# Top-k attention with a PReLU layer behind it: GpSimd's two row operations made one per tile, VectorE's product search moved by a slot

## The chip, the core and the metric

The kernel runs on one core of a Trainium2 chip. A core has a matrix engine (TensorE, in the profile PE, its weight loads PEld), VectorE (DVE), ScalarE (ACT), GpSimd (POOL), and SyncE (SP), whose instructions here only start DMAs. Each engine takes its instructions in program order and waits on semaphores where it needs what another engine makes. The metric is device time in microseconds (us): the median of a few executions. Before the change it is 826.78 us (three runs, 823.99 to 827.34).

## The reference

Two stages follow each other. Attention over 64 (batch, head) pairs, with 576 queries and 576 keys of 64 numbers each, in which every query keeps only the scores that are at least its 32nd largest:

```python
scores = scale * np.matmul(q, k.transpose(0, 1, 3, 2))
kth = np.partition(scores, -top_k, axis=-1)[..., -top_k:-top_k + 1]
mask = scores >= kth
scores = np.where(mask, scores, -1000000000.0)
scores = scores - np.max(scores, axis=-1, keepdims=True)
attn = np.exp(scores)
attn = attn / (np.sum(attn, axis=-1, keepdims=True) + 1e-09)
return np.matmul(attn, v)
```

Then a layer over 4608 tokens: `h = x @ w_in`, `g = max(h, 0) + alpha * min(h, 0)`, `out = g @ w_out`, with 512 inputs, 2048 hidden and 512 outputs.

## The kernel before

**Tiles.** The scores are made in tiles of 128 partitions with two rows of 576 scores on each. The code calls such a tile a duo: two rows (`i` = 0 and 1), each with a threshold of its own per partition. There are ND = 144 duos. One pass of the main loop (`for n in range(ND)`) is a slot, and in slot n every stage works on another duo, so that the duos run through the engines as through a pipeline. Two neighbouring duos 2m and 2m+1 form a group m, whose thresholds are found together.

**How a threshold is found.** ScalarE copies the scores of a duo out of PSUM into the tile `s` (`st_exit`). VectorE's MAX8 instruction gives the 8 largest of a row. It is run over six pieces of 96 scores of each row, 12 times for a duo. From these candidates, in odd slots, `fold`, `negate`, `least` and `turn` make a first threshold for the four rows of the group; it goes to column 0 of the tile `p9`. ScalarE counts the scores above it with a sign function whose sum is kept (`st_count`, tile `sg`, counts `cs`). GpSimd multiplies scores and signs (`st_y`, tile `y`), and VectorE's MAX8 over a row of `y` (`row(d, i)`) brings the 8 scores that lie next beside the threshold. With the count, three small VectorE instructions (`pick_steps`: `eq_`, `pk_`, `kt_`) pick the exact 32nd largest, and `kt_` writes it to columns of `KT`, which lies in the tile `KZ` of the profile. ScalarE then makes a penalty for every score below it (`st_relu`, tile `r`, which reads `KT`), GpSimd subtracts it from `s` in place, and ScalarE takes the exponential into the tile `w` (`st_exp`). A DMA transposes `w` into `wT`, and TensorE multiplies it with the values.

**What a slot does, in order, on each engine.** In slot n:

- ScalarE: sign of both rows of duo n-2; exponential of n-5; now and then a copy of finished output (`o_act`); penalty of both rows of n-4; exit of n+1; now and then a copy of transposed inputs (`qkT`).
- GpSimd: products of both rows of n-2; subtraction of both rows of n-4; in many slots a cast of values to bf16 (`cast_v`).
- VectorE, even slots: 12 MAX8 over duo n, with `eq_`, `pk_`, `kt_` of group (n-4)/2 behind the 2nd, 4th and 6th; the activation of the layer (`h_relu`, tile `gT`); row 0 of duo n-2; the reciprocal (`norm_a`); row 1 of duo n-2; the scaling of an attention output (`norm_b`); now and then a copy of transposed inputs.
- VectorE, odd slots: 12 MAX8 over duo n; `fold`, `h_relu`, `negate`; row 0 of duo n-2; `least`, `turn`; row 1 of duo n-2.
- TensorE: scores of duo n+1, attention output of an older duo, pieces of the layer, and matmuls over zeros (`rest<-idle`) where there is no work.

**What sets the order.** The order within each engine is that of the program text (class `Ordered`; the profile therefore puts nearly all instructions at line 32). What runs in which slot is a table by hand, `stage`, made from lags: `("count", 2)` means that duo d is counted in slot d+2, `("relu", 4)` that its penalty comes in slot d+4, `("exp", 5)` its exponential in slot d+5; picks of group m come in slot 2m+4. `dve_slot` is VectorE's part of a slot. In its present form it takes the rows from the table's `"count"` entries, that is in slot d+2. The scores of one duo lie in a single PSUM tile, so that TensorE makes the next scores only after the exit.

**Behind the loop** the last duos are finished in straight code: the last count and product of duo 142 (`st_count(D - 1)`, `st_y(D - 1)`), the picks of group 70, then `h_relu`, masks on VectorE for the last four duos (`st_mask`), and what is left of the layer.

Of the kernel before, what the change touches and what calls it, by code (L numbers as in the profile page):

```python
# [9 lines left out]
BF16 = mybir.dt.bfloat16  # L10
I32 = mybir.dt.int32
AF = mybir.ActivationFunctionType
ALU = mybir.AluOpType
# [3 lines left out]
BIG = float(2.0 ** 60)  # L17
# [42 lines left out]
def fast_path(tc, q, k, v, moe_w_in, moe_w_out, moe_alpha, out, flag):  # L60
    nc = tc.nc
    B, H, S, D = q.shape
# [9 lines left out]
    PE, ACT, DVE, POOL, SP = (  # L72
        Ordered(tc, e) for e in (nc.tensor, nc.scalar, nc.vector, nc.gpsimd, nc.sync)
    )
# [18 lines left out]
    with ExitStack() as ctx:  # L93
# [6 lines left out]
        two = pool("two", 2)  # L100
# [45 lines left out]
        def sm(ins, reads, writes):  # L146


            meet = lambda x, y: x == y if str in (type(x), type(y)) else x[0] < y[1] and y[0] < x[1]
            hit = lambda a, b: any(meet(x, y) for x in a for y in b)  # L150
            keep = [r[0] for r in recent
                    if hit(writes, r[1]) or hit(writes, r[2]) or hit(reads, r[2])]
            tc.declare_no_dep(ins.ins, group="small", keep=keep, reason="other columns")
            tc.add_to_no_dep_group("small", ins.ins)
            DVE.small.add(ins.ins.name)
            recent.append((ins.ins, reads, writes))
            del recent[:-60]
# [7 lines left out]
        KT = KZ[:, 0:2 * ND]  # L165
# [66 lines left out]
        T = {}  # L232
# [32 lines left out]
        def norm_of(n):  # L265

            return stage.get(("norm", n), 0)

        def pick_steps(m):

            def eq_():
                sm(DVE.tensor_tensor(eq, io9.unsqueeze(1).to_broadcast([128, 4, 9]),
                                     T.pop(("cs", m)).unsqueeze(2).to_broadcast([128, 4, 9]), ALU.is_equal),
                   [(292, 301)], [(256, 292)])

            def pk_():
                pk = T["pk"] = two.tile([128, 4, 9], FP32, name="pk", tag="pk")
                sm(DVE.scalar_tensor_tensor(out=pk, in0=eq, scalar=BIG, in1=T.pop(("p9", m)), op0=ALU.mult,
                                            op1=ALU.mult), [(256, 292), f"p9{m % 3}"], ["pk"])

            def kt_():
                sm(DVE.tensor_reduce(out=KT[:, 4 * m:4 * m + 4].unsqueeze(2), in_=T.pop("pk"),
                                     op=ALU.add, axis=AX.X), ["pk"], [])
            return [eq_, pk_, kt_]

        def row(d, i):
            DVE.max(out=T["p9", d // 2][:, 2 * (d % 2) + i, 1:9], in_=T["y", d][:, i, :])
# [29 lines left out]
        def dve_slot(n, f_late):  # L317

            norm = norm_of(n)
            rows = duos_at("count", n)  # L320
            picks = [f for m in duos_at("pick", n) for f in pick_steps(m)]
            s = T["s", n]
            if n % 2 == 0:
                T["up", n // 2] = two.tile([128, 4, NG // 2, 8], FP32, name="up", tag="up")
            up = T["up", n // 2]
            for i in range(2):
                r = 2 * (n % 2) + i
                for g in range(NG):
                    o = 24 * r + 8 * (g // 2)
                    m = DVE.max(out=(lo if g % 2 else up)[:, r, g // 2, :],  # L330
                                in_=s[:, i, GW * g:GW * g + GW])
                    if g % 2:
                        sm(m, [], [(o, o + 8)])
                        if picks:
                            picks.pop(0)()
            turn = None
            if n % 2:
                fold, negate, least, turn = threshold_steps(n // 2)
                fold()
                h_relu()  # L340
                negate()
            else:
                h_relu()
            for d in rows:
                row(d, 0)
            if turn:
                least()
                turn()
            if norm:
                norm_a(norm)  # L350
            for d in rows:
                row(d, 1)
            if norm:
                norm_b(norm)
            if f_late:
                h_pe()
                h_relu()
# [3 lines left out]
        def duos_at(kind, n):  # L361
            return stage.get((kind, n), [])

        for d in range(ND):
            for kind, lag in (("count", 2), ("relu", 4), ("exp", 5), ("av", 8 if d < 13 else 7)):
                stage.setdefault((kind, d + lag), []).append(d)
        for m in range(ND // 2):
            stage["pick", 2 * m + 4] = [m]
# [15 lines left out]
        def st_y(n):  # L384
            y = two.tile([128, 2, S], FP32, name="y", tag="y")
            sg = T.pop(("sg", n))
            for i in range(2):
                POOL.tensor_tensor(y[:, i, :], T["s", n][:, i, :], sg[:, i, :], ALU.mult)
            T["y", n] = y

        def st_relu(n, i):
            s = T["s", n]
            if i == 0:
                T["r", n] = two.tile([128, 2, S], BF16, name="r", tag="sg", bufs=3)
            r = T["r", n]
            ACT.activation(r[:, i, :], s[:, i, :], AF.Relu, bias=KT[:, 2 * n + i:2 * n + i + 1], scale=-BIG)
            POOL.tensor_tensor(s[:, i, :], s[:, i, :], r[:, i, :], ALU.subtract)

        def st_exp(n):
            w = ws[n % 3]  # L400
# [38 lines left out]
        def norm_a(n):  # L439
            rz = RZ[:, 2 * n - 2:2 * n + 2].rearrange("p (a h) -> p a h", a=2)  # L440
            DVE.reciprocal(rz, T["xo", n // 2][:, :, :, 64])
            T["rz"] = rz
# [112 lines left out]
        def h_relu(eng=None):  # L555
            if act:
                ch, f0, e_n, ph = act.pop(0)
                if eng is ACT:
                    ACT.activation(ch["g"][:, f0:f0 + e_n, :], ph, AF.Relu)
                else:  # L560
                    DVE.tensor_scalar(ch["g"][:, f0:f0 + e_n, :], ph, 0.0, None, ALU.max)
                ch["done"] += e_n
# [151 lines left out]
        for n in range(ND):  # L714
            now[0] = n
            run(n, "ld")
            o_sp()

            if not h_pe():
                keep_warm()  # L720
            wide_copy = n % 2 and (n, "prep") in todo
            if n > 3:
                run(n, "prep", 1)
            if n and on(n + 1):
                st_qk(n + 1)
            if n < 4:
                run(n, "prep", 2)
            for m in duos_at("av", n):
                st_av(m)
            late = len(hq) > (9 if n < 118 else 4) and n % 2 == 0  # L730

            for m in duos_at("count", n):
                st_count(m)
                st_y(m)
            for m in duos_at("exp", n):
                st_exp(m)
            if ready() > 4 or not wide_copy:
                o_act()
            did = o_pe()
            run(n, "w")  # L740

            dve_slot(n, late)
            for m in duos_at("relu", n):
                st_relu(m, 0)
                st_relu(m, 1)
            if on(n + 1):
                st_exit(n + 1)
            run(n, "cast")
            run(n, "lin_out")
            if (n, "lin") in todo:  # L750
                run(n, "lin")
            elif not ready() > 2 or not o_pe():
                if not did:
                    keep_warm()
            while pend:
                short = len(pend[0][0].shape) == 3
                wide = pend[0][0].shape[1] == 512
                on_dve = n > 3 and (short and n > 16 or wide and (n < 17 or n % 2 == 0))
                prep_evac(DVE.tensor_copy if on_dve else ACT.copy)
            if n == 1:  # L760
                sm(DVE.tensor_copy(alpha_ps, aps), [], [(304, 320)])
                ACT.activation(alpha1m, aps, AF.Copy, scale=-1.0, bias=1.0)
            run(n, "scale")
            if norm_of(n):
                st_xT(norm_of(n) - 1)
                st_xT(norm_of(n))

        def picked(m):
            for f in pick_steps(m):
                f()  # L770
            kv = T["kv", m] = two.tile([128, 4], FP32, name="kv", tag="kv")
            DVE.tensor_scalar(kv, KT[:, 4 * m:4 * m + 4], 1.0 / BIG, None, ALU.mult)
# [25 lines left out]
        D = ND - 1  # L798
# [5 lines left out]
        h_pe(2)  # L804
        st_count(D - 1)
        st_y(D - 1)
        picked(D // 2 - 1)
        h_relu()
        normed(D - 6)
# [46 lines left out]
        turn = 0  # L856
# [296 lines left out]
```

## Time and profile before

| what | value |
|---|---|
| median of three runs | 826.78 us |
| the profiled execution, its own time | 825.79 us |
| its span, first to last instruction | 823.8 us |
| granted TensorE clock, mean | 0.989 |

The profile is of a single execution. Its span is 2.0 us shorter than that execution's own time. The page gives busy time by engine, the chain of work that ended last, groups of equal instructions with their mean duration and the idle time before them, and DMA queues. Other views of the same trace list instructions in order of time, waits by who ended them, and busy time in chosen stretches. A row "x2" in a list by time is two instructions merged, with the time from the start of the first to the end of the last. On VectorE and ScalarE the recorded durations of neighbours overlap by some 0.1 us, so that the step from one start to the next is shorter than a duration.

### The profile page before, as it was taken

To read this page: it belongs to the slowest core of one execution; us is meant where nothing else is said; L and a number is where in the kernel's file an instruction comes from. 1 tells how busy PE (TensorE), PEld (TensorE's weight loads), DVE (VectorE), ACT (ScalarE), POOL (GpSimd) and SP (SyncE) were. 2 spreads that over 40 slices of the span, in tenths; PEclk is the share of its full clock that TensorE was granted. 3 is DMA by queue.
4 is the path that set the end of the run, shared out by engine and by line. 5 is a ranking of instruction groups with operands and counts; after the bars stand their busy time and mean duration, and the time that the engine had idled before them with its cause. 6 is when DMAs were issued, how large, how long until landed. Compare 5 with 4: busy or idle time off the path is not lost.

```text
span 823.8 us, 17880 instructions
## 1 busy us (share of the span) xinstructions
PE 742.5 (90%) x5422; PEld 424.1 (51%) x5422; DVE 760.5 (92%) x3474; ACT 763.4 (93%) x1258; POOL 745.4 (90%) x700
## 2 busy tenths in 40 slices
PE   8878889999899898998989898898989899989886
PEld 5333445555555555555545454455545555555554
DVE  3999989999999999999999999999999999999961
ACT  4999989999999999999999999999999998999921
POOL 1899989999998999999999999999999998999810
PEclk9999999999999999999999999999999999999989
DMA  6699977555666656556656556566666555544351
GB/s 138 171 184 179 176 132 144 104 121 116 123 131 125 122 102 139 109 130 124 132 109 141 112 94 142 119 135 113 117 134 123 123 93 110 92 88 87 69 119 43
DMA packets 344168, 100.21 MB, mean 122 GB/s; under 512 B 338032, under 2 KB 338048, under 8 KB 344064
## 3 DMA queue, kind: packets, MB, share of 16 engines
q1 hardware_dynamic: 340992, 91.87, 56.8%
q0 software_dynamic: 1872, 6.82, 3.5%
q8 instruction: 45, 0.74, 0.4%
q14 instruction: 59, 0.48, 0.2%
q10 hardware_dynamic: 1200, 0.30, 0.2%
HBM read 36.71 MB, written 9.44 MB: 56 GB/s over the span
## 4 chain that ended last, share of the span: by engine, by line
DVE 40%; ACT 19%; PE 19%; POOL 12%; issue 6%; DMA 2%; SPq 1%; ACTq 0%; POOLq 0%
DVE small L32 12%; DVE p L32 10%; DVE up L32 7%; POOL y L32 6%; ACT r L32 5%; POOL s_sb L32 5%; ACT sg L32 5%; PE ps_sc L32 5%; DVE gT L32 5%; ACT s_sb L32 4%; PE pz L32 4%; PE ph L32 4%; ACT w L32 3%; PE xo L32 2%; DVE qkT L32 2%
## 5 line engine op out<-in xcount | busy, mean ns | idle before, releaser
L32 POOL TENSOR_TENSOR y<-s_sb,sg 128x576 f32<-128x576 f32 x288 | 362.6, 1278 | 34.6 <-ACT sg L32 34.1
L32 POOL TENSOR_TENSOR s_sb<-s_sb,r 128x576 f32<-128x576 f32 x280 | 352.1, 1278 | 6.1 <-ACT r L32 5.8
L32 ACT ACTIVATE sg<-s_sb,p 128x576 bf16<-128x576 f32 x288 | 221.4, 773 | 6.9 <-DVE p L32 5.5
L32 DVE MAX8 up<-s_sb 128x8 f32<-128x96 f32 x864 | 212.6, 246 | 10.4 <-ACT s_sb L32 10.4
L32 DVE MAX8 p<-y 128x8 f32<-128x576 f32 x288 | 215.0, 748 | 6.4 <-POOL y L32 5.9
L32 DVE MAX8 small<-s_sb 128x8 f32<-128x96 f32 x864 | 216.8, 251 | 0.0
L32 PE MATMUL ps_sc<-qkT 64*128 64x512 f32 (+2 forms) x768 | 182.1, 563 | 23.2 <-ACT s_sb L32 23.1
L32 ACT ACTIVATE r<-s_sb,KZ 128x576 bf16<-128x576 f32 x280 | 201.0, 768 | 0.3 <-DVE KZ L32 0.3
L32 ACT COPY s_sb<-ps_sc 128x1152 f32<-128x1152 f32 x144 | 159.1, 1105 | 11.4 <-PE ps_sc L32 11.1
L32 ACT ACTIVATE w<-s_sb 128x1152 bf16<-128x1152 f32 x140 | 161.7, 1155 | 1.2 <-POOL s_sb L32 1.0
L32 PE MATMUL ph<-xT,w_in_b 128*128 128x256 bf16 (+1 forms) x1472 | 150.4, 250 | 6.8 <-DVE gT L32 3.3
L32 PEld LDWEIGHTS <-w_in_b 128*128 128x128 bf16 x1472 | 120.6, 98 | 50.0 <-issue 12.9
L32 PE MATMUL pz<-w_out_b,gT 128*128 128x512 bf16 x544 | 140.6, 381 | 0.4 <-DVE gT L32 0.4
L32 PE MATMUL xo<-v,wT 128*128 128x65 bf16 (+1 forms) x1560 | 123.4, 198 | 2.4 <-DMA wT<-w 2.1
L32 PEld LDWEIGHTS <-wT 128*128 128x128 bf16 (+3 forms) x1600 | 97.7, 100 | 32.7 <-DMA wT<-w 3.3
L32 DVE TENSOR_SCALAR gT<-ph 128x512 bf16<-128x512 f32 x137 | 92.5, 675 | 10.0 <-PE ph L32 10.0
L32 PEld LDWEIGHTS <-gT 128*128 128x128 bf16 x576 | 56.1, 98 | 71.1 <-issue 16.8
L32 PEld LDWEIGHTS ps_sc<-qkT 64*128 64x128 f32 (+1 forms) x768 | 55.3, 168 | 66.8 <-ACT s_sb L32 35.1
L32 PEld LDWEIGHTS ps_sc<-kd,qkT 128*128 128x128 f32 x256 | 38.3, 188 | 97.2 <-issue 94.9
L32 PE MATMUL pz<-w_lin_b,xT 128*128 128x512 bf16 x136 | 52.7, 388 | 15.7 <-ACT o_sb L32 15.5
L32 PE MATMUL ps_sc<-kd,qkT 128*128 128x128 f32 x256 | 62.9, 328 | 0.0
L32 PE MATMUL rest<-idle 128*128 128x512 bf16 x200 | 53.2, 394 | 7.4 <-DVE gT L32 5.4
(67 smaller groups left out, 604.5 us busy)
## 6 DMA issues: line engine op xcount, KB each, us to landing
k_st<-in_k_dram SPq DMA_DIRECT2D x64, 128.0 KB, 2.8
v_st<-in_v_dram SPq DMA_DIRECT2D x64, 128.0 KB, 2.7
q_st<-in_q_dram SPq DMA_DIRECT2D x62, 128.0 KB, 2.7
out_dram<-o_sb SPq DMA_DIRECT2D x31, 256.0 KB, 2.5
w_st<-in_moe_w_out_dram POOLq DMA_DIRECT2D x4, 1024.0 KB, 7.2
wT<-w SPq DMA_TRANSPOSE x144, 3.5
w_in_b<-in_moe_w_in_dram POOLq DMA_DIRECT2D x4, 512.0 KB, 5.8
k_st<-in_k_dram SPq DMA_DIRECT2D x32, 32.0 KB, 2.6
```

What stands on the lines that cost most here:

```text
L32: ins = self.tc.keep_in_program_order(f(*a, **kw))
```

## The change

GpSimd's products and subtractions each become one instruction over both rows of a duo, 1152 elements in place of twice 576. The product thus starts when the signs of both rows are there, the subtraction when both penalties are, and what follows waits for the whole tile. The two penalties stay two instructions of ScalarE, now next to each other in the program text, ahead of the one subtraction.

VectorE's rows get an entry of their own in the table, `("row", 3)`: duo d is searched in slot d+3. In an odd slot the two rows of duo n-3 take the places of those of duo n-2. In an even slot both rows stand at the head, ahead of the 12 MAX8 and the picks that are among these. Behind the loop the two rows of duo 141, which now fall past its end, are added ahead of the picks of group 70.

```diff
@@ dve_slot(n, f_late)
-            rows = duos_at("count", n)
+            rows = [(d, i) for d in duos_at("row", n) for i in range(2)]
...
             up = T["up", n // 2]
+            if n % 2 == 0:
+                for d, i in rows:
+                    row(d, i)
             for i in range(2):
                 r = 2 * (n % 2) + i
                 for g in range(NG):
...
-            turn = None
             if n % 2:
                 fold, negate, least, turn = threshold_steps(n // 2)
                 fold()
                 h_relu()
                 negate()
+                for d, i in rows[:1]:
+                    row(d, i)
+                least()
+                turn()
+                for d, i in rows[1:]:
+                    row(d, i)
             else:
                 h_relu()
-            for d in rows:
-                row(d, 0)
-            if turn:
-                least()
-                turn()
             if norm:
                 norm_a(norm)
-            for d in rows:
-                row(d, 1)
-            if norm:
                 norm_b(norm)
...
-            for kind, lag in (("count", 2), ("relu", 4), ("exp", 5), ("av", 8 if d < 13 else 7)):
+            for kind, lag in (("count", 2), ("row", 3), ("relu", 4), ("exp", 5), ("av", 8 if d < 13 else 7)):
...
@@ st_y, st_relu
-            for i in range(2):
-                POOL.tensor_tensor(y[:, i, :], T["s", n][:, i, :], sg[:, i, :], ALU.mult)
+            POOL.tensor_tensor(y, T["s", n], sg, ALU.mult)
             T["y", n] = y
-        def st_relu(n, i):
+        def st_relu(n):
             s = T["s", n]
-            if i == 0:
-                T["r", n] = two.tile([128, 2, S], BF16, name="r", tag="sg", bufs=3)
-            r = T["r", n]
-            ACT.activation(r[:, i, :], s[:, i, :], AF.Relu, bias=KT[:, 2 * n + i:2 * n + i + 1], scale=-BIG)
-            POOL.tensor_tensor(s[:, i, :], s[:, i, :], r[:, i, :], ALU.subtract)
+            r = two.tile([128, 2, S], BF16, name="r", tag="sg", bufs=3)
+            for i in range(2):
+                ACT.activation(r[:, i, :], s[:, i, :], AF.Relu, bias=KT[:, 2 * n + i:2 * n + i + 1], scale=-BIG)
+            POOL.tensor_tensor(s, s, r, ALU.subtract)
...
@@ behind the loop
         st_y(D - 1)
+        row(D - 2, 0)
+        row(D - 2, 1)
         picked(D // 2 - 1)
```

More of the change, by code (lines that the diff above doesn't have):

```diff
@@ L386, in st_y @@
             sg = T.pop(("sg", n))
-            for i in range(2):
-                POOL.tensor_tensor(y[:, i, :], T["s", n][:, i, :], sg[:, i, :], ALU.mult)
-            T["y", n] = y
-        def st_relu(n, i):
-            s = T["s", n]
-            if i == 0:
-                T["r", n] = two.tile([128, 2, S], BF16, name="r", tag="sg", bufs=3)
-            r = T["r", n]
-            ACT.activation(r[:, i, :], s[:, i, :], AF.Relu, bias=KT[:, 2 * n + i:2 * n + i + 1], scale=-BIG)
-            POOL.tensor_tensor(s[:, i, :], s[:, i, :], r[:, i, :], ALU.subtract)
+            POOL.tensor_tensor(y, T["s", n], sg, ALU.mult)
+            T["y", n] = y
+        def st_relu(n):
+            s = T["s", n]
+            r = two.tile([128, 2, S], BF16, name="r", tag="sg", bufs=3)
+            for i in range(2):
+                ACT.activation(r[:, i, :], s[:, i, :], AF.Relu, bias=KT[:, 2 * n + i:2 * n + i + 1], scale=-BIG)
+            POOL.tensor_tensor(s, s, r, ALU.subtract)
         def st_exp(n):
@@ L743, in fast_path @@
             for m in duos_at("relu", n):
-                st_relu(m, 0)
-                st_relu(m, 1)
+                st_relu(m)
             if on(n + 1):
```

## The prediction

> **What bounds the kernel now.** I read the page's busy times first, then two stretches of the span.
>
> ```profile
> PE 742.5 (90%) x5422; PEld 424.1 (51%) x5422; DVE 760.5 (92%) x3474; ACT 763.4 (93%) x1258; POOL 745.4 (90%) x700
> 300.00:400.00 100.00, 91.58 (x657) 52.40 (x653) 99.00 (x468) 99.51 (x164) 99.32 (x91) 1.00 0.58 119
> 30.00:60.00 30.00, 23.73 (x134) 10.47 (x134) 28.11 (x120) 29.65 (x52) 29.70 (x32) 1.00 0.81 169
> by line: POOL s_sb L32 41.9%; POOL y L32 40.8%; POOL v L32 8.3%; issue 7.4%; ACT sg L32 2.9%; POOL w_in_b L32 2.0%; POOL w_st L32 0.1%; POOLq L32 0.1%
> ```
>
> The stretch rows give length, then busy time of PE, PEld, DVE, ACT and POOL. In 300 to 400 us VectorE, ScalarE and GpSimd are all at 99%. Relieving GpSimd alone can therefore shorten little, while any new wait of ScalarE or VectorE lengthens the span at once. Only in 30 to 60 us is GpSimd alone the chain (last row: the chain of waits there).
>
> Two slots, even and odd, make a period. I cut the span where ScalarE starts the penalty (r) in even slots, and let the stretch view give each period's length. The 62 periods from slot 16 to slot 140 fall into four classes, here by first and last row: 13 near 9.95 us (129.4 us together), 18 near 10.30 (185.5), 9 from 10.37 to 10.58 (94.3), 22 from 10.61 up (248.3).
>
> ```profile
> 168.45:178.40 9.95, 9.95 (x71) 5.68 (x71) 9.71 (x47) 9.94 (x17) 9.61 (x9) 1.00 0.53 105
> 748.76:758.71 9.95, 9.47 (x87) 5.69 (x85) 9.63 (x46) 9.94 (x18) 9.95 (x9) 1.00 0.32 61
> ...
> 101.27:111.57 10.30, 10.30 (x63) 5.19 (x63) 9.41 (x47) 10.30 (x19) 10.30 (x11) 1.00 0.92 145
> 738.46:748.76 10.30, 9.31 (x87) 5.75 (x85) 10.23 (x50) 10.30 (x19) 10.12 (x9) 1.00 0.47 103
> ...
> 210.38:220.96 10.58, 10.43 (x72) 6.01 (x72) 10.31 (x48) 9.95 (x18) 9.98 (x10) 1.00 0.87 162
> 662.49:673.04 10.55, 9.39 (x65) 5.26 (x65) 10.48 (x49) 10.41 (x18) 10.55 (x11) 1.00 0.52 89
> ...
> 111.57:124.10 12.53, 10.38 (x58) 5.06 (x59) 9.02 (x45) 10.44 (x19) 10.44 (x10) 0.86 0.69 120
> 717.84:728.51 10.67, 10.21 (x87) 6.05 (x87) 10.03 (x48) 10.40 (x18) 10.67 (x11) 1.00 0.62 100
> sum 657.44, PE 605.75 PEld 348.31 DVE 637.44 ACT 643.73 POOL 639.98; mean PE 9.77 PEld 5.62 DVE 10.28 ACT 10.38 POOL 10.32
> ```
>
> In short and middle periods ScalarE (fourth busy time) has no idle time. Here is one short period by time:
>
> ```profile
> 410.21 1.44 ACT L32 ACTIVATE r<-s_sb,KZ 128x576 bf16<-128x576 f32 x2
> 411.55 1.11 ACT L32 COPY s_sb<-ps_sc 128x1152 f32<-128x1152 f32 x1
> 412.69 0.26 DVE L32 MAX8 up<-s_sb 128x8 f32<-128x96 f32 x1 [0.26 <-ACT s_sb L32]
> ...
> 417.38 0.17 DVE L32 TENSOR_SCALAR p<-small 128x4 f32<-128x4 f32 x1
> 417.46 0.75 DVE L32 MAX8 p<-y 128x8 f32<-128x576 f32 x1
> 417.58 0.78 ACT L32 ACTIVATE sg<-s_sb,p 128x576 bf16<-128x576 f32 x1
> ...
> 418.13 0.24 DVE L32 MAX8 up<-s_sb 128x8 f32<-128x96 f32 x1
> 419.12 1.15 ACT L32 ACTIVATE w<-s_sb 128x1152 bf16<-128x1152 f32 x1
> 419.28 2.51 POOL L32 TENSOR_TENSOR y<-s_sb,sg 128x576 f32<-128x576 f32 x2
> 419.29 0.17 DVE L32 TENSOR_REDUCE KZ<-pk 128x4 f32<-128x36 f32 x1
> 420.17 1.43 ACT L32 ACTIVATE r<-s_sb,KZ 128x576 bf16<-128x576 f32 x2
> ```
>
> A ring runs through it: penalty and exit on ScalarE (410.21 to 412.66), the odd slot of VectorE (412.69 to 418.13, 5.44), the even slot's head up to KT (418.13 to 419.46, 1.33), and the next penalty at 420.17. KT is ready 0.71 us before ScalarE asks for it. This slack decides the case.
>
> **The change part by part.** (a) *Both rows at the head of even slots.* They stand ahead of the 12 MAX8 and so ahead of KT. One row costs 0.67 on VectorE (417.46 to 418.13), two 1.34. KT comes 1.34 later in the same slot, and the slack is 0.71. The odd slot keeps two rows, so its 5.44 stays. The ring becomes 2.48 (410.21 to 412.69) + 5.44 + 1.34 + 1.33 + 0.02 for the handover = 10.61 us a period, whatever ScalarE has to do. Behind the waiting penalty ScalarE queues the exit, on which the next odd slot of VectorE and the next scores on TensorE hang; so the delay stays in the ring. Each period becomes the longer of its present length and 10.61:
>
> - 13 × 10.61 − 129.4 = 8.5
> - 18 × 10.61 − 185.5 = 5.5
> - 9 × 10.61 − 94.3 = 1.2
> - 22 longer ones: 0
>
> Together +15.2 us. Before slot 16 ScalarE has weights to scale besides, and periods are longer than the ring, so I count 0 there; one, from start to start of r:
>
> ```profile
> 43.48 1.43 ACT L32 ACTIVATE r<-s_sb,KZ 128x576 bf16<-128x576 f32 x2
> ...
> 54.96 1.42 ACT L32 ACTIVATE r<-s_sb,KZ 128x576 bf16<-128x576 f32 x2
> ```
>
> (b) *Waits that go.*
>
> ```profile
> ACT sg L32 <- DVE p L32: 4.4, 10, 0.8
> ...
> DVE p L32 <- POOL y L32: 5.9, 13, 1.2
> ...
> ACT r L32 <- DVE KZ L32: 0.3, 1, 0.3
> ```
>
> In even slots VectorE no longer ends with two rows, so it reaches the odd slot earlier and the threshold (turn) is less often late for the signs: of the 4.4 us (slots from 100 to 760 us) one, 0.63, lies in the short period at 210.38, which (a) lifts anyway; I take −3.5, bounds 0 and −4.4. Rows searched a slot later find y ready (the 5.9 of the whole span), but in the ring that gives only slack.
>
> (c) *GpSimd's merged instruction* does not occur in this trace. Rows around it:
>
> ```profile
> L32 POOL TENSOR_TENSOR s_sb<-s_sb,r 128x576 f32<-128x576 f32 x280 | 352.1, 1278 | 6.1 <-ACT r L32 5.8
> L32 POOL CAST v<-v_st 128x256 bf16<-128x256 f32 x64 | 25.2, 397 | 0.0
> L32 POOL CAST v<-v_st 64x128 bf16<-64x128 f32 x32 | 9.2, 288 | 0.0
> L32 ACT COPY o_sb<-pz x34: 559/562/585, 168.0 to 817.3; 128x512 f32<-128x512 f32 x34
> ```
>
> Upper bound 2 × 1278 = 2.56 us, nothing saved. The casts give (397 − 288)/128 = 0.85 ns an element and a fixed 179 ns; if all of that is saved once, 2.38. As two now take 2.51 with an overlap, I take 2.45: −0.06 a merge. It counts where GpSimd is the chain, 12 merges in the 30 to 60 us and a few after: −1 us, bounds 0 and −3. Elsewhere it hides behind the ring of (a). The coarser handover costs nothing as long as this path is shorter: penalties 1.44, subtraction 2.45, product 2.45, subtraction 2.45, three handovers 0.09, exponential 1.05 (419.12 to 420.17) = 9.93; a cast (0.39) makes it 10.32, below 10.61. With an output copy on ScalarE as well (0.56 recorded, some 0.47 without the overlap) it is 10.79; few periods have both and nothing else.
>
> The Trainium skill (GPSIMD Engine Reference, section 3.1) puts a two-input operation at about 2.5 cycles an element at 1.2 GHz. By that 576 elements are 1.20 us of the recorded 1.278, and a merge would take an estimated 2.48 us and save only 0.03 of the 2.51: with it, this term is −0.4 in place of −1.
>
> (d) *Behind the loop.* Rows of duo 141 now stand ahead of the picks, and whatever follows on VectorE is later:
>
> ```profile
> 777.47 0.76 ACT L32 ACTIVATE sg<-s_sb,p 128x576 bf16<-128x576 f32 x1
> 777.64 2.52 POOL L32 TENSOR_TENSOR y<-s_sb,sg 128x576 f32<-128x576 f32 x2
> 777.85 1.08 DVE L32 TENSOR_SCALAR kv<-KZ 128x4 f32<-128x4 f32 x1
> 778.85 0.68 DVE L32 TENSOR_SCALAR gT<-ph 128x512 bf16<-128x512 f32 x1
> 779.58 1.05 PE L32 MATMUL ph<-xT,w_in_b 128*128 128x128 bf16 x16 [2.06 <-DVE gT L32]
> L32 DVE TENSOR_SCALAR kv<-KZ x2: 170/626/1081, 777.9 to 788.9; 128x4 f32<-128x4 f32 x2
> ```
>
> Two rows, 1.34. And kv took 1.08 beside the product, 0.17 the other time. It ended when the first product's instruction did; now the product starts with the second sign's end (778.23) and runs as one to about 780.7, and if kv waits as long, gT starts at 780.7, not 778.85. TensorE waits for gT here, so the end moves by the same: +2, bounds 1.3 and 2.5. The Trainium skill (SBUF — State Buffer, "Who interferes with whom") tells why: VectorE and GpSimd share a port pair that one instruction holds to its end. The 1.08 agrees.
>
> Sum on the profiled execution's own 825.8 us (span 823.8 and 2.0 around it): 15.2 − 3.5 − 1 + 2 = +12.7, so 838.5. That execution lies 1.0 below the median shown; I say 839.
>
> **The rivals.**
>
> *GpSimd's relief decides, faster.* For it: the chain leans on GpSimd.
>
> ```profile
> DVE 40%; ACT 19%; PE 19%; POOL 12%; issue 6%; DMA 2%; SPq 1%; ACTq 0%; POOLq 0%
> ```
>
> 12% of 823.8 are 99 us, 40 pairs of 2.5 us; at 0.06 each −2.4 (−5.6 at the lower bound), and the 5.9 of row waits: 825.8 − 8.3 = about 817.5. It decides only if KT has 1.34 us to spare in even slots, that is if VectorE came to them at least 0.6 earlier. Against it: VectorE is 99% busy and starts its odd slot on the exit.
>
> *Long periods pay for short ones, no change.* Across all 62 periods, the longer of 10.61 and ScalarE's own busy time comes to 662, only 4.5 over the 657.4. The 22 long ones hold 12.5 us of ScalarE's idle time, mostly waits for TensorE. If these shrink when all else is later: 825.8 + 4.5 − 1 + 1 = 830. Against it: such a wait lies within the ring (exit) or follows it, and comes on top.
>
> *The coarse handover decides as well, slower still.* At 2.56 us the path of (c) with a cast is 10.65, with an output copy 11.1: up to 0.5 over the ring in about 17 periods (half of the 34 copies fall in even slots), +8: 847. For it: GpSimd at 99%; against: the copies fall mostly in periods that are long already.
>
> That the change doesn't do what it says is out: the order of its instructions is fixed by the program text.
>
> **How the numbers follow.** Forecast 0.68, slower still 0.12, no change 0.11, faster 0.09. Within 0.5% (4.1 us) a measurement of this kernel can't tell a change. The first two are slower by more; of no change (830, near the edge at 830.9) I put 0.08 within and 0.03 beyond, of faster 0.08 and 0.01. So faster 0.08, same 0.09, slower 0.83. Range 828 to 848: the sum with all terms at their low ends and part of the absorption, up to the coarse handover.
>
> **What would show it.** ScalarE's wait of r for KZ, now 0.3 us in all, grows to 12 to 20 in some 40 places; short periods become 10.6; waits of sg for p fall below 2; merged GpSimd instructions take 2.38 to 2.56, and its busy time falls by about 15; kv behind the loop takes over 1.5. Wrong if r never waits for KZ, or if periods stay at 9.95.

## The result and the profile after

The changed kernel takes 846.12 us (median of four runs, 844.70 to 847.55), the one before 826.29 (four runs, 823.99 to 827.34): ratio 1.0255, 95% interval 1.0236 to 1.0274. The change makes the kernel slower, by 19.8 us where 12.7 were forecast. The profiled execution spans 843.2 us against 823.8, 19.4 more.

The page after, busy time by engine, then the chain of work that ended last by engine:

```profile
PE 736.8 (87%) x5340; PEld 424.1 (50%) x5422; DVE 766.6 (91%) x3474; ACT 771.9 (92%) x1258; POOL 711.1 (84%) x416
...
DVE 52%; ACT 21%; PE 11%; issue 8%; DMA 3%; POOL 3%; SPq 1%; ACTq 0%; DVEq 0%; POOLq 0%
```

GpSimd lost 34.3 us of work (745.4 to 711.1) and its share of the chain fell from 12% to 3%, VectorE's rose from 40% to 52%. So the relief came as meant, and the end moved to VectorE. The merged instructions, from the page's groups (busy us, mean ns of one, idle before):

```profile
L32 POOL TENSOR_TENSOR y<-s_sb,sg 128x1152 f32<-128x1152 f32 x144 | 342.4, 2378 | 65.9 <-ACT sg L32 53.2
L32 POOL TENSOR_TENSOR s_sb<-s_sb,r 128x1152 f32<-128x1152 f32 x140 | 332.6, 2376 | 31.2 <-ACT r L32 24.9
```

The view of waits after (us in total, times, longest):

```profile
DVE up L32 <- ACT s_sb L32: 25.5, 43, 3.1
...
PE ph L32 <- DVE gT L32: 22.7, 26, 4.1
...
ACT s_sb L32 <- PE ps_sc L32: 14.0, 9, 3.5
...
ACT r L32 <- DVE KZ L32: 11.4, 29, 0.6
...
ACT sg L32 <- DVE p L32: 3.7, 7, 1.0
...
DVE p L32 <- POOL y L32: 0.9, 1, 0.9
```

The penalty r, which waited 0.3 us in all for KZ, now waits 29 times, and never more than 0.6: a small wait that comes back every period. VectorE in turn waits for the exit (`up` for `s_sb`) 25.5 us instead of 10.4, as these lines of before show, with the wait of the signs for the threshold beside it:

```profile
DVE up L32 <- ACT s_sb L32: 10.4, 19, 3.1
...
ACT sg L32 <- DVE p L32: 5.5, 11, 1.1
```

Both engines wait for each other within one period, which is how a ring shows. Here is one by time, the counterpart of the short period shown of before:

```profile
419.27 1.44 ACT L32 ACTIVATE r<-s_sb,KZ 128x576 bf16<-128x576 f32 x2
...
420.62 1.09 ACT L32 COPY s_sb<-ps_sc 128x1152 f32<-128x1152 f32 x1
...
421.75 0.26 DVE L32 MAX8 up<-s_sb 128x8 f32<-128x96 f32 x1 [0.41 <-ACT s_sb L32]
...
426.52 2.07 DVE L32 MAX8 p<-y 128x8 f32<-128x576 f32 x3
...
428.51 0.25 DVE L32 MAX8 up<-s_sb 128x8 f32<-128x96 f32 x1
...
429.67 0.17 DVE L32 TENSOR_REDUCE KZ<-pk 128x4 f32<-128x36 f32 x1
...
429.88 1.44 ACT L32 ACTIVATE r<-s_sb,KZ 128x576 bf16<-128x576 f32 x2 [0.51 <-DVE KZ L32]
```

Three searches stand in one row: the last of the odd slot and the two that now open the even slot. From r to r are 10.61 us. The stretch view by periods (length, then busy PE, PEld, DVE, ACT, POOL), cut at the start of r in even slots as before; shown are one of the many at 10.60 (767.43), two near 10.70 (101.24, 235.48), two that became longer (123.06, 213.47), and the sum of all 62:

```profile
101.24:111.93 10.69, 10.43 (x65) 5.38 (x67) 9.60 (x47) 10.49 (x18) 10.34 (x7) 1.00 0.91 153
...
123.06:137.23 14.17, 11.97 (x79) 6.64 (x78) 10.20 (x48) 10.53 (x18) 10.17 (x7) 0.88 0.76 152
...
213.47:224.88 11.41, 11.07 (x74) 6.30 (x75) 10.73 (x49) 10.12 (x17) 9.89 (x6) 1.00 0.88 148
...
235.48:246.18 10.70, 9.17 (x65) 5.19 (x64) 10.60 (x49) 10.54 (x18) 9.96 (x6) 1.00 0.60 119
...
767.43:778.03 10.60, 9.70 (x84) 5.85 (x85) 10.09 (x48) 10.07 (x16) 9.92 (x5) 1.00 0.36 69
sum 676.77, PE 603.78 PEld 349.31 DVE 645.13 ACT 651.45 POOL 611.02; mean PE 9.74 PEld 5.63 DVE 10.41 ACT 10.51 POOL 9.86
```

The sum grew from 657.44 to 676.77: these 62 periods hold the whole 19.4. The stretch ahead of them (first r of slot 16 at 101.27 before, 101.24 after) and the one behind them did not change:

```profile
778.03:843.20 65.17, 51.14 (x496) 34.09 (x500) 38.69 (x124) 32.38 (x52) 24.38 (x13) 0.93 0.37 78
```

The same stretch before, from its last cut to the end of the span:

```profile
758.71:823.80 65.09, 52.62 (x505) 34.05 (x503) 39.13 (x120) 32.03 (x53) 25.71 (x22) 0.94 0.37 80
```

By the forecast's four classes:

| periods before | sum before | sum after | gained or lost | forecast |
|---|---|---|---|---|
| 13 near 9.95 | 129.4 | 137.9 | +8.5 | +8.5 |
| 18 near 10.30 | 185.5 | 191.6 | +6.1 | +5.5 |
| 9 from 10.37 to 10.58 | 94.3 | 97.3 | +3.0 | +1.2 |
| 22 from 10.61 up | 248.3 | 250.0 | +1.7 | −3.5 |

### The profile page after: what moved, and what is told of

It reads as the page before. It is cut to its first block, busy times and chain, and to the rows that moved or that the text cites. A ratio compares the mean times of both kernels' runs of the same rounds, so it can differ in the third digit from the quotient of the medians.

```text
span 843.2 us, 17583 instructions
## 1 busy us (share of the span) xinstructions
PE 736.8 (87%) x5340; PEld 424.1 (50%) x5422; DVE 766.6 (91%) x3474; ACT 771.9 (92%) x1258; POOL 711.1 (84%) x416
## 4 chain that ended last, share of the span: by engine, by line
DVE 52%; ACT 21%; PE 11%; issue 8%; DMA 3%; POOL 3%; SPq 1%; ACTq 0%; DVEq 0%; POOLq 0%
DVE p L32 17%; DVE small L32 15%; DVE up L32 9%; ACT s_sb L32 7%; ACT r L32 7%; DVE gT L32 5%; ACT sg L32 4%; PE ph L32 3%; PE pz L32 3%; PE ps_sc L32 2%; ACT w L32 2%; DMA wT<-w 2%; DVE bot L32 1%; POOL y L32 1%; DMA q_st<-in_q_dram 1%
## 5 line engine op out<-in xcount | busy, mean ns | idle before, releaser
L32 POOL TENSOR_TENSOR y<-s_sb,sg 128x1152 f32<-128x1152 f32 x144 | 342.4, 2378 | 65.9 <-ACT sg L32 53.2
L32 POOL TENSOR_TENSOR s_sb<-s_sb,r 128x1152 f32<-128x1152 f32 x140 | 332.6, 2376 | 31.2 <-ACT r L32 24.9
L32 DVE MAX8 up<-s_sb 128x8 f32<-128x96 f32 x864 | 212.9, 246 | 25.5 <-ACT s_sb L32 25.5
L32 ACT ACTIVATE r<-s_sb,KZ 128x576 bf16<-128x576 f32 x280 | 200.9, 765 | 13.0 <-DVE KZ L32 11.4
L32 PE MATMUL ps_sc<-qkT 64*128 64x512 f32 (+2 forms) x768 | 184.0, 569 | 26.9 <-ACT s_sb L32 26.7
L32 DVE MAX8 p<-y 128x8 f32<-128x576 f32 x288 | 204.2, 749 | 1.0 <-POOL y L32 0.9
L32 PE MATMUL ph<-xT,w_in_b 128*128 128x256 bf16 (+1 forms) x1472 | 151.8, 251 | 23.6 <-DVE gT L32 22.7
L32 PE MATMUL pz<-w_out_b,gT 128*128 128x512 bf16 x523 | 135.9, 379 | 8.4 <-issue 6.0
L32 PE MATMUL rest<-idle 128*128 128x512 bf16 x187 | 49.9, 380 | 9.7 <-DVE gT L32 6.6
L32 ACT ACTIVATION_READ_ACCUMULATOR sg<-s_sb,p 128x1 f32 x288 | 55.0, 191 | 0.0
```

Source lines behind the costliest of these rows:

```text
L32: ins = self.tc.keep_in_program_order(f(*a, **kw))
```

## The experiments

Two theories stood at the start. A: the ring through KT sets the period, because both rows stand ahead of the picks. B: GpSimd's coarser handover does. Theories C, D and E came up on the way. The median of before was 824.63 us in the runs of the first four kernels, 824.96 in those of the next four, 825.76 in those of the last four; ratios are to these.

| kernel | us | ratio | interval |
|---|---|---|---|
| before, merged only (e1) | 870.42 | 1.0552 | 1.0533 to 1.0571 |
| after, not merged (e2) | 844.81 | 1.0242 | 1.0223 to 1.0262 |
| rows split by duo, merged (e3) | 850.32 | 1.0319 | 1.0293 to 1.0344 |
| rows split by duo, not merged (e4) | 829.14 | 1.0054 | 1.0036 to 1.0071 |
| after, one search more at the head (e5) | 888.44 | 1.0746 | 1.0711 to 1.0781 |
| after, activation late in odd slots (e7) | 860.11 | 1.0433 | 1.0411 to 1.0455 |
| after, picks a slot later (e8) | 842.31 | 1.0211 | 1.0181 to 1.0240 |
| e8, activation late in odd slots (e9) | 854.76 | 1.0369 | 1.0346 to 1.0392 |
| e1 with the threshold ahead of the rows (e10) | 841.16 | 1.0210 | 1.0184 to 1.0236 |
| after, activation early (e11) | 844.45 | 1.0223 | 1.0208 to 1.0238 |
| before, threshold ahead of the rows (e12) | 825.77 | 0.9999 | 0.9988 to 1.0009 |
| before, only the subtraction merged (e13) | 830.63 | 1.0060 | 1.0045 to 1.0075 |

### The two halves of the change, each alone (e1, e2)

e1 is the kernel before with GpSimd's part of the change; e2 is the kernel after with GpSimd's part taken back.

```diff
-            for i in range(2):
-                POOL.tensor_tensor(y[:, i, :], T["s", n][:, i, :], sg[:, i, :], ALU.mult)
+            POOL.tensor_tensor(y, T["s", n], sg, ALU.mult)
...
-            POOL.tensor_tensor(s[:, i, :], s[:, i, :], r[:, i, :], ALU.subtract)
+            POOL.tensor_tensor(s, s, r, ALU.subtract)
```

> GpSimd's merged instructions alone, VectorE's rows where they were before. Theory A (the ring through KT makes the loss; it is 10.6 us because two rows stand ahead of KT): the ring stays at 9.3 us, so short periods stay below 10.3 and the loss of 19 us is not here. But rows are searched in the slot in which the product is made, and a whole product ends some 1.1 us later than its first half did: VectorE should wait for y far more than the 5.9 us of before. Between -2 and +8 us, ratio 0.998 to 1.010. Theory B (the coarse handover makes the loss): most of the loss is here, ratio 1.015 to 1.025.

> VectorE's rows moved as in the change, GpSimd's instructions two per duo as before. Theory A: short periods become 10.60 to 10.61 us as in the change, total within 4 us of the changed kernel, ratio 1.020 to 1.030. Theory B: close to the kernel before, ratio 0.997 to 1.005.

e2 costs all that the whole change costs. Its view of waits, and in the stretch view the first of its 31 periods of 10.60 or 10.61 us:

```profile
ACT r L32 <- DVE KZ L32: 15.3, 43, 0.6
```

```profile
147.43:158.03 10.60, 10.54 (x83) 5.76 (x83) 9.74 (x45) 10.42 (x19) 10.54 (x11) 1.00 0.47 90
```

The moved rows alone make the ring, with two GpSimd instructions a duo. The merge on top of them changes nothing that can be told: 846.12 against 844.81, with overlapping intervals (1.0236 to 1.0274, 1.0223 to 1.0262). Theory B falls for this change.

e1 missed by far: it is 45.8 us slower, where theory A gave at most 8 and theory B 12 to 21. Its waits, and one period by time (slot 134):

```profile
DVE p L32 <- POOL y L32: 60.9, 77, 3.0
...
ACT sg L32 <- DVE p L32: 38.5, 58, 1.8
```

```profile
771.70 2.37 POOL L32 TENSOR_TENSOR y<-s_sb,sg 128x1152 f32<-128x1152 f32 x1 [0.61 <-POOL s_sb L32]
...
774.10 0.76 DVE L32 MAX8 p<-y 128x8 f32<-128x576 f32 x1 [0.72 <-POOL y L32]
...
775.83 0.25 DVE L32 MAX8 up<-s_sb 128x8 f32<-128x96 f32 x1
...
779.35 0.75 DVE L32 MAX8 p<-y 128x8 f32<-128x576 f32 x1
...
780.51 0.17 DVE L32 TENSOR_SCALAR p<-small 128x4 f32<-128x4 f32 x1
...
780.71 0.78 ACT L32 ACTIVATE sg<-s_sb,p 128x576 bf16<-128x576 f32 x1 [0.78 <-DVE p L32]
...
782.47 2.37 POOL L32 TENSOR_TENSOR y<-s_sb,sg 128x1152 f32<-128x1152 f32 x1 [1.10 <-issue]
```

This is a second ring, through the threshold. The product (771.70) must be whole before VectorE's rows of the even slot (774.10); behind them come the odd slot (775.83), its row 0 (779.35), the threshold (780.51), the signs (780.71) and the next product of an even duo (782.47): 10.77 us from product to product. Searching a row one slot later cuts exactly this ring, as the row no longer waits for the product just made. So the two halves of the change belong together: 45.8 for the merge alone, 20.2 for the later rows alone, 19.8 for both. What is left is the price of the later rows.

### Where in the second ring the merge pays (e10, e12, e13)

Theory D: the merge alone costs because the threshold stands behind a row's search that waits for the whole product. e10 is e1, e12 the kernel before, each with the threshold ahead of row 0; e13 is the kernel before with only the subtraction merged.

```diff
-            for d in rows:
-                row(d, 0)
             if turn:
                 least()
                 turn()
+            for d in rows:
+                row(d, 0)
```

> GpSimd's merge alone (rows searched in the slot of their product), but in odd slots the threshold stands ahead of both rows. Theory D (the merge alone costs 45 us because row 0 waits for the whole product and the threshold is queued behind this wait, so the next signs and with them the next product are late: a ring sign, product, row, threshold, sign): waits of sg for p fall from 38 us to under 10, and the loss falls to 10 to 25 us, as rows still wait for y in even slots. Rival: the loss of the merge alone comes from exponentials waiting for whole subtractions, which this leaves as it was: ratio 1.045 to 1.060.

> The kernel before, with the threshold (least, turn) ahead of the first row in odd slots; nothing merged, nothing a slot later. The signs' waits for the threshold are 5.5 us in the kernel before and row 0 takes 0.67. Theory D (the order in which a row's search can hold up the threshold costs): those waits nearly go, ratio 0.993 to 0.999. Rival (they lie in periods that wait for something else as well): 0.999 to 1.003.

> The kernel before, with GpSimd's two subtractions of a duo made one and its two products left as they are. Theory D (the merge alone cost 45 us because VectorE's first row waits for the whole product, with the threshold queued behind it): the product is handed over row by row as before, so nearly none of that comes: ratio 0.995 to 1.010. Rival (GpSimd's later start and end of any merged instruction costs): the subtraction carries about half of the 45 us, ratio 1.02 to 1.03.

e10 takes one row's search, 0.67, out of the second ring. Two of its periods in which ScalarE has no further copy and is not full, in the stretch view:

```profile
742.39:752.58 10.19, 8.72 (x77) 5.14 (x75) 9.88 (x47) 10.00 (x17) 9.44 (x5) 1.00 0.35 67
763.03:773.20 10.17, 9.56 (x86) 5.76 (x84) 9.86 (x47) 9.99 (x18) 9.42 (x5) 1.00 0.21 40
```

These stand near 10.18, against 10.77 in e1. Eight others without a further copy stand at 9.97 to 10.01, where ScalarE is full; their like in e1 stood at 10.47 to 10.56. 29 us of the 45.8 are back, and the signs' wait for the threshold falls from 38.5 to 11.3, where under 10 was expected. e13 keeps the product in two instructions and costs 4.9 us; if the two parts add up, some 41 of the 45.8 belong to the merged product. Both fit theory D. e12 gains nothing, against what theory D gave for it (0.993 to 0.999): with two products a duo the threshold's place does not matter, although signs wait 5.5 us for it before. In e12 they still do:

```profile
ACT sg L32 <- DVE p L32: 5.3, 15, 1.1
```

So these waits do not hang on row 0 alone. This matters for the forecast below.

### The same rows with a shorter ring (e3, e4)

The rows of odd duos stay at the head of even slots; those of even duos go back to their own slot, behind the activation. An odd slot has no rows any more: four searches a period as before, but the ring through KT is shorter by two.

```diff
-            for kind, lag in (("count", 2), ("row", 3), ...
+            for kind, lag in (("count", 2), ("row", 2 if d % 2 == 0 else 3), ...
...
             if n % 2 == 0:
                 for d, i in rows:
-                    row(d, i)
+                    if d % 2:
+                        row(d, i)
...
             else:
                 h_relu()
+                for d, i in rows:
+                    if d % 2 == 0:
+                        row(d, i)
```

> The change with one difference: rows of even duos are searched in slot d+2, behind the activation at the end of even slots, rows of odd duos stay at the head of even slots in slot d+3; odd slots hold no rows. Two rows still stand at the head of even slots, but the odd slot is shorter by two (1.34 us), so the ring is 10.61 - 1.34 = 9.27 us. Theory A: short periods fall below 10.3 us, bounded by ScalarE (9.95) and VectorE's own work (10.2 to 10.6), and TensorE waits for gT less than the 22.7 us of the change; ratio to before 0.990 to 1.006. Theory B, or a theory that rows at the head of even slots cost as such: ratio 1.015 and more.

> The same order of rows as the run before it, but GpSimd's instructions two per duo as in the kernel before. Tells what the merge is worth when the ring does not bind. Theory A: ScalarE or VectorE bind, GpSimd at two instructions (5.0 us a slot with casts) is just as full as before, so the merge is worth 0 to 6 us: ratio to before 0.992 to 1.008, at or above the merged one. Theory B: the handover is finer here, so this one is faster than the merged one.

e4 (not merged) runs at 829.14, 15.7 below e2 and 4.5 above the kernel before, and its short periods are back where they were before; one of them:

```profile
189.09:199.06 9.97, 9.74 (x72) 5.74 (x71) 9.83 (x46) 9.95 (x18) 9.53 (x10) 1.00 0.56 120
```

In e4 two rows stand at the head too, and r waits for KZ 0.4 us in all. Rows at the head hold up KT only when what follows the exit in the odd slot is long as well. e3 (merged) costs 21.2 more than e4. It misses theory A's range (0.990 to 1.006), and that the one with two instructions is faster is what theory B said of this pair: the handover does cost where a row is searched in the slot of its product, as the even duos' rows are here. They wait for the whole product 18.3 us, where in e4 they wait 4.1. The waits of e3:

```profile
DVE p L32 <- POOL y L32: 18.3, 18, 3.0
...
ACT sg L32 <- DVE p L32: 12.6, 25, 1.5
```

### A measured dose (e5)

```diff
+        def again(rows):
+            for d, i in rows[:1]:
+                spare8 = two.tile([128, 8], FP32, name="spare8", tag="spare8")
+                DVE.max(out=spare8, in_=T["y", d][:, i, :])
...
             if n % 2 == 0:
+                again(rows)
                 for d, i in rows:
                     row(d, i)
```

> The kernel after, with one more search of a row of y (its result is not used) at the head of even slots, ahead of the rows. Theory A (the ring through KT sets the period): the ring grows by one row, 0.66 us, from 10.60 to 11.26. Every period of two slots that is now 10.60 becomes 11.26, also those whose ScalarE has a copy more; with every period of the kernel after, slots 16 to 140, as the longer of its present length and 11.27, their sum grows by 31 us (676.8 to 707.9): 877 us, ratio 1.059 to 1.068. Rival (VectorE's total work per period sets it, wherever it stands): the same 0.66 in each of 62 periods, 41 us, long ones too: 887, ratio 1.074. Rival (GpSimd's handovers set it): below 855.

Its waits, and in the stretch view two of 32 periods of 11.26 or 11.27 us and two of 21 from 11.35 to 11.37:

```profile
ACT r L32 <- DVE KZ L32: 53.0, 66, 1.2
```

```profile
106.98:118.34 11.36, 10.63 (x69) 5.38 (x69) 10.27 (x48) 10.49 (x18) 10.36 (x7) 1.00 1.02 147
...
156.40:167.66 11.26, 10.93 (x89) 6.11 (x88) 10.95 (x50) 10.50 (x19) 10.91 (x7) 1.00 0.44 84
...
679.13:690.49 11.36, 10.96 (x95) 6.64 (x94) 11.26 (x50) 10.51 (x18) 9.46 (x6) 1.00 0.41 86
...
797.48:808.74 11.26, 8.93 (x82) 5.51 (x81) 10.75 (x49) 10.55 (x18) 9.05 (x5) 1.00 0.44 95
```

In the 32 the period is theory A's to the hundredth, 10.60 + 0.66 = 11.26, and there VectorE has 0.3 us or more to spare (10.95 and 10.75 busy): it is the ring and not its work. In 20 of the 21 others VectorE is 11.24 to 11.27 busy and has only 0.1 to spare: there its own work fills the period, as that rival has it. The total, 888.44, is 11 above theory A's and falls on the number of the rival that charges every period. By the cuts, 36.3 of the 42.7 us between the profiled spans lie in the 62 periods (713.1 against 676.8), where A's sum was 31; the first r of slot 16 comes 5.7 later, at 106.98. That fill was left out of the expectation.

### Opening the ring with picks a slot later (e8)

For duos below 130, picks, penalty, exponential and attention output come one slot later, with seven score buffers (smaller tiles were reused to make room); in even slots the rows stand behind the activation, in odd slots the threshold ahead of them. GpSimd stays merged.

```diff
-            for kind, lag in (("count", 2), ("row", 3), ("relu", 4), ("exp", 5), ("av", 8 if d < 13 else 7)):
+            for kind, lag in (("count", 2), ("row", 3), ("relu", 4 + sh(d)), ("exp", 5 + sh(d)),
+                              ("av", (8 if d < 13 else 7) + sh(d))):
...
-            stage["pick", 2 * m + 4] = [m]
+            stage["pick", 2 * m + 4 + sh(2 * m)] = [m]
```

> The change with the ring opened: picks, penalty, exponential and what follows come one slot later for duos below 130 (picks now in odd slots), one more buffer for the scores, rows behind the activation in both kinds of slots, and the threshold ahead of the rows in odd slots. KT is then a slot's length from the exit that it depends on. Theory A: no wait of r for KT, short periods are bounded by ScalarE (9.95 to 10.3 us), the merged GpSimd instructions cost nothing because their rows are searched a slot later; ratio to before 0.985 to 1.003. Theory B or a loss through rows searched a slot later as such: 1.01 and more.

842.31 us is a miss as a total; the ratio lies where theory B, or a loss through later rows as such, was to put it. The stretch view from the exit of slot 16 to that of slot 120 tells more, the same 104 exits in three kernels. Before:

```profile
102.60:653.88 551.28, 506.61 (x3684) 290.17 (x3683) 535.46 (x2492) 540.43 (x886) 537.81 (x488) 1.00 0.62 122
```

After:

```profile
102.59:668.09 565.50, 503.56 (x3629) 290.25 (x3683) 541.45 (x2490) 546.88 (x886) 513.05 (x280) 1.00 0.61 120
```

e8:

```profile
102.40:656.09 553.69, 510.79 (x3673) 288.81 (x3671) 541.39 (x2486) 543.62 (x884) 512.20 (x280) 0.99 0.61 122
```

In the steady part 11.8 of the 14.2 us are back, with merge and later rows both in place, and r waits for KZ only 0.2 us from 102 to 656 us: the ring was the price. e8 changes more than the picks (the places of rows and threshold, one more buffer), and what each of these gives was not measured. What e8 loses, it loses behind this stretch (span 840.7 against 823.8), around the switch back to early picks at duo 130, where ScalarE waits 2.8 us for scores and VectorE 2.3 for TensorE, and behind the loop. A better end was not tried.

### The place of the activation (e7, e9, e11)

Theory C: the long periods are longer than forecast because the activations, and so TensorE's free buffers, come at uneven distances; e7 moves the odd slot's activation behind the threshold, e9 does so in e8. Theory E: they come too late; e11 moves them earlier with the ring as long as it is.

e7, the same lines in e9 (where no row stands ahead of `least`):

```diff
                 fold()
-                h_relu()
                 negate()
                 for d, i in rows[:1]:
                     row(d, i)
                 least()
                 turn()
+                h_relu()
```

e11 (in even slots `had` says that there were picks):

```diff
                         if picks:
                             picks.pop(0)()
+                            if n % 2 == 0 and not picks:
+                                h_relu()
...
+                h_relu()
                 fold()
-                h_relu()
                 negate()
...
-            else:
+            elif not had:
                 h_relu()
```

> The change, but in odd slots VectorE's activation (gT) stands behind the threshold (turn) and not ahead of it. The ring through KT holds the same instructions and stays 10.60 us. In the change the activation of even slots comes 1.34 us later, so that activations are unevenly spaced (some 5.6 us from odd to even, 4 from even to odd), and TensorE waits 22.7 us for gT in place of 3.3. Theory C (the rest of the loss, long periods, is this uneven spacing: TensorE gets its PSUM buffer back late and the scores come late): the wait of TensorE's ph for gT falls to 10 us or less, short periods stay at 10.6, total 3 to 7 us below the changed kernel, ratio to before 1.015 to 1.022. Rival: the long periods have other causes (transposes landing late), ratio 1.022 to 1.028 as in the change.

> As the run before it, with the activation of odd slots behind the threshold as well, so that the threshold comes 0.6 us earlier. If signs waiting for the threshold (4 to 5 us in the kernel before) are what is left above ScalarE's busy time, 2 to 4 us below the run before it; if waits for TensorE are what is left, the same within 2 us. Ratio to before 0.980 to 1.003.

> The kernel after, with the activation (gT) earlier on VectorE at the same length of the ring: in even slots right behind KT, about 1.0 us earlier, in odd slots ahead of the fold, about 0.7 earlier. Theory E (the 4 to 5 us by which the long periods miss the forecast come from TensorE, whose buffers for the layer are freed later when rows stand ahead of the activation): short periods stay at 10.60, the wait of ph for gT falls from 22.7 us to below 12, and the time falls by 3 to 7 us against the kernel after: ratio 1.016 to 1.022. Rival (only the ring counts, or the later fold costs as much): 1.022 to 1.028.

e7 is 14.0 us slower than the kernel after, e9 12.4 slower than e8. In e7 TensorE's wait for gT does fall, from 22.7 to 14.8, though not to 10, and the time rises all the same: theory C falls. How the late activation costs was not followed; what the trace of e7 shows is that r waits for KZ 22.2 us in place of 11.4. In e9 the signs' wait for the threshold falls from 7.5 to 1.4, as meant, and gains nothing. For theory E, the waits of e11:

```profile
ACT s_sb L32 <- PE ps_sc L32: 17.2, 8, 4.7
...
ACT r L32 <- DVE KZ L32: 11.6, 28, 0.6
...
PE ph L32 <- DVE gT L32: 6.5, 5, 4.5
```

TensorE's wait for gT falls from 22.7 to 6.5 as expected, and 32 periods stay at 10.60 or 10.61, yet the median falls by 1.7 us only, not 3 to 7, and the intervals against before overlap (1.0208 to 1.0238; after 1.0236 to 1.0274). The profile of e11 is of an execution of 854.9 us, 10 above its median, so these waits and periods are not its usual ones to the tenth. Theory E explains at most a small part.

## Why the prediction was right, and where it was off

**(a) Both rows at the head of even slots: right.** The ring was forecast at 10.61 and measured at 10.60 to 10.61. The short class came out at +8.5 as forecast, the middle one at +6.1 for 5.5. Most of the difference comes from periods at 10.70 in which VectorE has a wide copy of transposed inputs: it is 10.60 busy there, as in the row at 235.48, and waits for nothing from one KT to the next, so that its own work takes the ring's place. The forecast took the longer of the ring and the present length, and left VectorE's own work out. The class from 10.37 up gave +3.0 for 1.2, because two periods of it, 213.47 (10.58 before, 11.41 after) and 677.34 (10.55 before, 11.39 after), got waits that reach TensorE. e2, e5 and e8 show the ring three ways: rows alone, a dose, and the ring opened.

**(b) Waits that go: the mis-sized step.** It said −3.5, on the ground that VectorE reaches the odd slot earlier when the even slot no longer ends with rows. It gains little there: the odd slot begins with the exit, as the forecast's own ring says, and VectorE merely waits for it longer (25.5 us for 10.4). So the signs' wait fell only from 5.5 to 3.7 over the span, and e12 shows that not even a threshold 0.67 earlier removes it. Where the wait did go, the period did not always follow: the one at 441.78 lost 0.53 of it and went from 11.34 to 11.30. On the whole the 22 long periods grew by 1.7 us. Slots 18 and 20 carry that much alone: 23.56 us together before, 25.29 after. Among the others eight between 10.90 and 11.18 fell to 10.85 or 10.86, 1.5 together, and the two at 673.04 and 684.43 grew by 1.5. At 123.06 the chain of waits of the kernel after runs through a transposing DMA to the attention output and the scores behind it:

```profile
121.02 5.54 DMA wT<-w
126.61 0.79 PE xo L32 x10
```

Of the 6.7 us between forecast (12.7) and profile (19.4), this term makes 5.2, the two classes of (a) 0.6 and 1.8, and (c) and (d) together −0.9. Why just these periods take longer is not settled; e11 speaks against late activations being most of it.

**(c) GpSimd's merge: the instruction cheaper than taken, the gain not there.** One instruction takes 2.377 us, the forecast's lower bound of 2.38 and not the 2.45 taken. Of the recorded durations the casts' fixed 179 ns is saved whole: 2 × 1278 − 2377 = 179. As the two took 2.51 from start to end, a merge saves 0.13 in time. The Trainium skill (GPSIMD Engine Reference, section 2.1, and not 3.1 as the forecast has it) led to an estimated 2.48; the measurement decides, 2.38. The gain of 1 us in the fill did not come (101.27 to 101.24), although each merge saved more than thought. The step that failed is that GpSimd alone sets the pace from 30 to 60 us: ScalarE was 29.65 of these 30 us busy before, and after the change it has the chain of waits there:

```profile
by line: ACT r L32 22.6%; ACT sg L32 18.8%; ACT w_out_b L32 14.2%; issue 13.3%; ACT s_sb L32 12.2%; ACT w L32 10.7%; POOL s_sb L32 8.0%; DVE small L32 1.1%; DVE up L32 1.1%; ACT qkT L32 0.5%; DVE KZ L32 0.3%; DVE pk L32 0.3%; ACTq L32 0.1%
```

That the coarse handover costs nothing here was right: e2 and the kernel after can't be told apart. What the forecast did not see is that the later search is what hides it; without it the merge costs 45.8.

**(d) Behind the loop: right in the mechanism, not in the price.** kv was to wait for the whole product, and does, 1.67 us for 1.08:

```profile
798.65 1.67 DVE L32 TENSOR_SCALAR kv<-KZ 128x4 f32<-128x4 f32 x1
```

gT starts 22.20 us behind the last cut in place of 20.14, about as forecast. But the end did not move with it: 65.09 us from the last cut to the end before, 65.17 after, where +2 was forecast. The step that failed is that the end moves by what gT is late: the last run of `pz` matmuls, 15 of them in the chain of waits, starts 55.72 us behind the cut in place of 55.31. Where in between the delay is made up was not followed. That (c) and (d), −1 and +2 in the forecast, both came to nothing and nearly cancel is luck for the sum.

**The rivals.** GpSimd's relief took 34 us of work off that engine and no time off the kernel. Long periods did not pay for short ones, they added to them. The coarse handover had the right number, 847, and the wrong mechanism: e2 has no merge and takes 844.8. Two sums of the rivals are slightly off, and no chance hangs on them: 661.65 − 657.44 is 4.2 and not 4.5, and 40 merges at 0.13 each save 5.2 and not 5.6.

**The signs named beforehand.** r waits for KZ 11.4 us in 29 places, where 12 to 20 in some 40 were named (15.3 in 43 with two instructions a duo, e2). Part of the ring shows at VectorE's end instead, as its wait for the exit. Short periods at 10.60, merged instructions of 2.38 us and a kv of over 1.5 us came as named. The signs' wait for the threshold did not fall below 2 (3.7), and GpSimd's busy time fell by 34.3 us where about 15 were named.

## What to carry to other kernels

When engines stand at 99%, look for the rings that close over a period before costing an edit by busy time: add up the work from one start of an instruction to its next over all engines, and treat each edit as a change of a ring's length. An edit that relieves one ring, as a later search relieves the one through the threshold, may lengthen another, as it does the one through KT; the period is the longest of them. An instruction moved earlier or later frees time only if the next instruction on its engine does not start on something else in the same ring.

## What the runs showed of the hardware beside this

A GpSimd instruction over 576 elements a partition was recorded with 1278 ns and one over 1152 with 2377: 1.908 ns an element and, worked out from the two, a fixed 0.18 us. A VectorE instruction of four elements (kv) took 0.17 us without a GpSimd product beside it, 1.08 beside a product of 576 and 1.67 beside one of 1152, and ended with that product both times. The Trainium skill (SBUF — State Buffer, "Who interferes with whom") says that the instruction that has the port pair of VectorE and GpSimd holds it to its end, and both numbers agree with it. Not every small instruction waits so: the threshold's (`turn`, 128x4 as well) took 0.17 us at 417.38 before, in the middle of two subtractions that ran from 416.46 to 418.97. What makes the difference no run here shows.
